# Sending a spectrum swap by halves of the frequencies, under an order of instructions searched one by one

## The chip, the cores and the metric

The kernel runs on one core of a Trainium2 chip. Times are device microseconds (us). With one core there is no second die to compare with; a run counts as slow when it is over 1.5% above the fastest of its kernel. Ratios are the mean time of one kernel's fast runs over the mean time of the other's fast runs of the same rounds, so they are not quite the ratios of the medians that stand beside them. The first comparison and three batches of experiments ran at different times, the batches on three chips; kernels of different batches are compared through their ratios to before. A +- beside such a difference is worked out from the two 95% intervals.

Engines are called TensorE (PE in the profile; PEld is its weight load), VectorE (DVE), ScalarE (ACT), GpSimd (POOL) and SyncE (SP, which issues the DMAs).

## The reference, cut to what matters

Two layers, each a gated long convolution (A) and an MLP (B), on x of 2048 x 512:

```python
def _A_ref(q, k, v, shift_k, ssm_k, ssm_D):
    k_shift = sum over 4 taps of k shifted in time * shift_k      # short filter
    kv = k_shift * v
    y = irfft(rfft(kv, 2*S) * rfft(ssm_k, 2*S))[:S] + kv * ssm_D   # long convolution over time
    return q * y
def _B_ref(x, w1, b1, w2, b2):
    return gelu(_layernorm(x) @ w1 + b1) @ w2 + b2

x = A_q
x = x + _A_ref(_layernorm(x), A_k, A_v, ...)   # y depends on k and v alone
x = x + _B_ref(_layernorm(x), ...)
x = x + _A_ref(_layernorm(x), A_k, A_v, ...)   # the same y again
x = x + _B_ref(_layernorm(x), ...)
```

The convolution y does not depend on x, so the kernel computes it once, in its first 90 us; the rest is the two MLPs.

## The kernel before: the parts that matter

A Python program lists about 1,080 operations with their data, and a list scheduler, at build time, puts them in an order on each engine and picks the engine of those that may run on ScalarE or VectorE (the evacuations of PSUM to SBUF). The order that it picks is then fixed: each engine runs its list in sequence and waits on semaphores.

The scheduler's knobs before: one bias per group of operations, and one reluctance of VectorE per group.

```python
    BIAS = {'fir0': 47900, 'fir1': -42700, ... 'z8': -60900}          # cut: one per group
    SHY = {'fir0': 1000, 'fir1': 150, 'h1': 950, ... 'z2': 1000}      # cut
    ...
            o.prio = o.base + o.extra + self.BIAS.get(o.tag, 0.0) + (1e9 - 1e5 * o.i if o.dma else 0.0)
```

The convolution is a two-stage Fourier transform made of matmuls. Stage 1 of the long filter (group h1), then stage 2 (h2), which leaves the filter's spectrum H with real parts in 64 partitions and imaginary parts in the other 64. A complex product also needs a copy HS with the two halves of the partitions exchanged. That copy is the *swap*: 4 MB from SBUF to SBUF, 16 DMAs of 256 KB.

```python
    P.tag = "h2"
    for k8 in range(16):                       # 8 of the 128 first-stage frequencies each
        tl = stage2(R_G, range(8 * k8, 8 * k8 + 8), 128)
        evac(BOTH, A(0, 128, R_H + 32 * k8, [4, 8], [512, 32], [1, 4]), ...)
    for d0, n in PARTS:                        # channels 0 to 63, 64 to 127
        for g in range(2):                     # upper half to lower, lower half to upper
            for c in range(0, 128 * n, 2048):
                src, dst = [A(64 * p, 64, r + 128 * d0 + c, [1, 2048]) for p, r in ((g, R_H), (1 - g, R_HS))]
                dma(dst, src, 1 << 18, reads=[src], rate=210.0)
```

A row of such a DMA (4096 bytes of one partition) holds all 128 frequencies, so no row can go before all 16 stage-2 evacuations are done. Meanwhile the short filter runs (fir0 and fir1 on TensorE, fir2 and fir3 as 16 multiplications and additions of 128x2048 on VectorE), then stage 1 of its result (x1), stage 2 (x2) and the products with H and HS on VectorE, 16 of 128x2048:

```python
            x = A(0, 128, xo, [0, 2], [4 * nk, n // 4], [1, 4 * nk])
            h = A(0, 128, R_H + 128 * d0 + 4 * k0, [R_HS - R_H, 2], [512, n // 4], [1, 4 * nk])
            tt(h, x, h, ALU.mult, 30 + 1.09 * w)        # reads H and HS: waits for the swap
```

The inverse stages (i1, i2) and the first normalisations lead to the MLP.

Of the kernel before, what the change touches and what calls it, by code (L numbers as in the profile page):

```python
# [12 lines left out]
PE, ACT, DVE, POOL, SP = "tensor", "scalar", "vector", "gpsimd", "sync"  # L13
# [25 lines left out]

class Op:  # L40
    __slots__ = ("i", "engs", "eng", "fn", "dur", "preds", "succ", "prio", "tile", "dma", "start", "end",
                 "pos", "inc", "waits", "val", "npred", "ready", "bytes", "base", "extra", "gate", "tag")


class Prog:
# [3 lines left out]

    G = 4  # L50
    LAT = 155.0
    BIAS = {'fir0': 47900, 'fir1': -42700, 'fir2': 66400, 'fir3': -218300, 'h1': 4900, 'h2': 147100, 'ht': 209900, 'i1_0': -157900, 'i1_64': 58800, 'i2_0': -83000, 'i2_64': -41700, 'm1': 127100, 'm2': -35800, 'q0': -48300, 'q1': 45200, 'q19': 14700, 'q2': -92900, 'q20': -190100, 'q21': 90800, 'q22': -36400, 'q3': -100900, 'q4': -92500, 'q5': 39100, 'q6': 114300, 'q7': 58300, 'q8': -27800, 'warm': -27900, 'warm0': 88600, 'x1_0': -97300, 'x1_1': 141900, 'x1_2': 44000, 'x1_3': -57400, 'x2_0': 149200, 'x2_64': 106500, 'y0': 55200, 'y1': 72900, 'y19': -31000, 'y2': 63100, 'y20': -119200, 'y21': 86900, 'y22': -58600, 'y3': -58100, 'y4': 64900, 'y5': 173000, 'y6': 55800, 'y7': -62200, 'y8': 8200, 'z0': 79600, 'z1': 62900, 'z19': 54600, 'z2': -30600, 'z20': 40700, 'z21': -55300, 'z22': -26300, 'z3': -7000, 'z4': 5000, 'z5': -87400, 'z6': -97200, 'z7': -15700, 'z8': -60900}
    SHY = {'fir0': 1000, 'fir1': 150, 'h1': 950, 'h2': 0, 'ht': 150, 'i1_0': 300, 'i1_64': 600, 'i2_0': 0, 'i2_64': 300, 'x1_0': 150, 'x1_1': 310, 'x1_2': 300, 'x1_3': 1000, 'x2_0': 360, 'x2_64': 1010, 'z0': 3000, 'z1': 600, 'z2': 1000}

    def __init__(self, nc):
        self.nc = nc
# [124 lines left out]
    def schedule(self):  # L181
        ops = self.ops
        n = len(ops)
        for o in ops:
            o.succ = []
            o.npred = len(o.preds)
            o.ready = 0.0
        for o in ops:
            for p in o.preds:
                ops[p].succ.append(o.i)  # L190
        for o in reversed(ops):
            d = o.dur if isinstance(o.dur, (int, float)) else min(o.dur.values())
            if o.dma:
                d += 2000.0 + o.bytes / 370.0
            b = 0.0
            for s in o.succ:
                b = max(b, ops[s].base + (0 if ops[s].engs == o.engs else self.LAT))
            o.base = b + d
            o.prio = o.base + o.extra + self.BIAS.get(o.tag, 0.0) + (1e9 - 1e5 * o.i if o.dma else 0.0)
        self.banks = [(0.0, []) for _ in range(8)]  # L200
        free = {e: 0.0 for e in (PE, ACT, DVE, POOL, SP)}
        ready = {e: [] for e in free}
        self.order = {e: [] for e in free}
        for o in ops:
            if o.npred == 0:
                for e in o.engs:
                    ready[e].append(o)
        done = 0
        dma_free = 0.0
        t = 0.0  # L210
        while done < n:
            best = None
            for e in free:
                te = max(free[e], 0.0)
                cand = None
                for o in ready[e]:
                    if o.eng is not None or any(g.eng is None for g in o.gate):
                        continue
                    s = max(te, o.ready)
                    new = [x for x in o.tile if x.base is None]  # L220
                    if any(x.pool.gate and self._gated(x) for x in new):
                        continue
                    if new:
                        pl = self._place(new, s)
                        if pl is None:
                            continue
                        s = pl[0]
                    k = (s + (self.SHY.get(o.tag, 300.0) if e == DVE and len(o.engs) > 1 and o.dur[DVE] > o.dur[ACT] else 0.0), -o.prio, o.i)
                    if cand is None or k < cand[0]:
                        cand = (k, o, s)  # L230
                if cand is None:
                    continue
                o = cand[1]
                d = o.dur if isinstance(o.dur, (int, float)) else o.dur[e]
                if best is None or (cand[0][0], cand[0][0] + d) < best[0]:
                    best = ((cand[0][0], cand[0][0] + d), e, o, cand[2])
            if best is None:
                raise RuntimeError("no op can be scheduled: %s" % [(o.i, e, [(t.base, t.left) for t in o.tile]) for e in ready for o in ready[e]][:10] + str((done, n)))
            _, e, o, s = best
            d = o.dur if isinstance(o.dur, (int, float)) else o.dur[e]  # L240
            o.eng, o.start = e, s
            new = [x for x in o.tile if x.base is None]
            if new:
                for tl, base in self._place(new, s)[1]:
                    tl.base = base
                    tl.pool.used += 1
                    for b in range(base, base + tl.pool.nb):
                        for p in self.banks[b][1]:
                            if p.i not in o.preds:
                                o.preds[p.i] = "psum"  # L250
                        self.banks[b] = None
            for tl in o.tile:
                tl.left -= 1
            free[e] = s + d
            if o.dma:
                dma_free = max(dma_free, s + d) + o.bytes / 370.0
                o.end = dma_free + 1900.0
            else:
                o.end = s + d
            for tl in o.tile:  # L260
                if tl.left == 0:
                    tail = [p for p in tl.ops if p.eng != PE] or [tl.ops[-1]]
                    tl.pool.used -= 1
                    for b in range(tl.base, tl.base + tl.pool.nb):
                        self.banks[b] = (max(p.end for p in tail) + self.LAT, tail)
            o.pos = len(self.order[e])
            self.order[e].append(o)
            for x in o.engs:
                ready[x].remove(o)
            for si in o.succ:  # L270
                q = ops[si]
                lat = self.LAT
                if not o.dma and len(q.engs) == 1 and q.engs[0] == o.eng:
                    lat = 0.0 if o.eng == PE or q.preds[o.i] == "psum" else 50.0
                q.ready = max(q.ready, o.end + lat)
                q.npred -= 1
                if q.npred == 0:
                    for x in q.engs:
                        ready[x].append(q)
            done += 1  # L280
        self.length = max(o.end for o in ops)
# [148 lines left out]
PARTS = ((0, 64), (64, 64))  # L430
# [5 lines left out]
def bass_interleave_layers__ssm_conv_h3__mixer_channel_mlp__prompt_kernel(  # L436
# [7 lines left out]
    def A(p0, n, off, *dims):  # L444
        return bass.AP(ar, p0 * AR + off, [[AR, n]] + [list(d) for d in dims])
# [16 lines left out]
    pos = [0]  # L462
# [17 lines left out]
    R_HRAW, R_HP, R_H = R_1, R_1 + 8192, R_1  # L480
    R_G, R_HS = R_4, R_2
# [19 lines left out]
    def dma(dst, src, nbytes, reads=(), prio=0.0, writes=None, eng=SP, rate=370.0):  # L501
        return P.op(eng, lambda e: e.dma_start(dst, src, allow_slow_non_contiguous=True), 550.0, reads=reads,  # L502
                    writes=[dst] if writes is None else writes, dma=True, nbytes=nbytes * 370 / rate, prio=prio)
# [34 lines left out]
    for i in range(NDV):  # L538
        o, s = A(0, 128, R_SJ + 512 * i, [128, 4], [1, 128]), A(0, 128, R_SR + 512 * DV_CH[i], [1, 4], [4, 128])
# [43 lines left out]
    for i, c in enumerate(PE_CH):  # L583
        o, a = A(0, 128, R_DG + i * 512, [128, 4], [1, 128]), A(0, 128, R_ID, [0, 4], [1, 128])
        tt(o, a, A(0, 128, R_SR + 512 * c, [1, 4], [4, 128]), ALU.mult, 1200.0, POOL)
    P.tag = "ht"
    for b in range(4):
        tl = Tile(dconv)
        src = [A(0, 128, R_HRAW + b * 2048 + a, [16, 128]) for a in range(16)]
# [8 lines left out]
        o = A(0, 1, R_HP + b * 2048, [64, 32], [1, 4])  # L598
# [33 lines left out]
    for k8 in range(16):  # L632
        tl = stage2(R_G, range(8 * k8, 8 * k8 + 8), 128)
        evac(BOTH, A(0, 128, R_H + 32 * k8, [4, 8], [512, 32], [1, 4]),
             lambda tl=tl: Q(tl, 0, 128, 0, [128, 8], [4, 32], [1, 4]), E1, tl)
    for d0, n in PARTS:
        for g in range(2):
            for c in range(0, 128 * n, 2048):
                src, dst = [A(64 * p, 64, r + 128 * d0 + c, [1, 2048]) for p, r in ((g, R_H), (1 - g, R_HS))]
                dma(dst, src, 1 << 18, reads=[src], rate=210.0)  # L640


    P.tag = ""

# [326 lines left out]
```

## Time and profile before

| what | before |
|---|---|
| time, median (first comparison, 4 runs) | 247.13 us |
| span of the profiled run | 245.5 us |
| first filter multiplication on VectorE (k has landed) | 17.44 us |
| swap issued from | 39.49 us |
| first MLP matmul | 89.06 us |
| TensorE busy from there to the end | 152.5 us of 156.4 us |

The page of before. The digits are the busy tenths of 40 slices of 6.1 us each:

```profile
span 245.5 us, 5643 instructions
## 1 busy us (share of the span) xinstructions
PE 228.3 (93%) x2382; PEld 154.6 (63%) x2399; DVE 175.1 (71%) x361; ACT 140.9 (57%) x222; POOL 34.1 (14%) x71
...
PE   7968789896799989999999999999999999999994
...
DVE  0759999999898898889999967998687203002233
ACT  2297898999898997665455343633265130872000
...
GB/s 240 372 408 406 406 47 82 215 212 212 346 396 198 0 3 0 45 43 3 46 43 43 3 41 67 24 1 21 101 53 0 109 19 43 45 0 43 43 45 85
```

Slices 15 and later are the MLPs, where TensorE is full. Slices 2 to 14 are the convolution, where three engines are nearly full. In slices 6 and 7 (31 to 43 us) the DMA rate drops to 47 and 82 GB/s: the loads are done and the swap cannot start. Then it runs at about 212 GB/s.

The DMA queue's own timeline of before (start, duration, queue, what, how many):

```profile
39.49 17.66 SPq L502 DMA_DIRECT2D ar<-ar  x16
```

VectorE's timeline of before: start, duration, what, and in brackets the idle time just before and what ended it. L513 is the helper of all SBUF multiplications and additions, L519 that of the evacuations:

```profile
17.44 6.90 DVE L513 TENSOR_TENSOR ar<-ar 128x2048 bf16<-128x2048 bf16 x6 [1.81 <-DMA ar<-in_A_k_dram]
...
53.29 9.16 DVE L513 TENSOR_TENSOR ar<-ar 128x2048 bf16<-128x2048 bf16 x8
63.63 9.17 DVE L513 TENSOR_TENSOR ar<-ar 128x2048 bf16<-128x2048 bf16 x8 [1.18 <-DMA ar<-ar]
...
79.10 1.23 DVE L519 CAST ar<-ps 128x1024 bf16<-128x1024 f32 x1 [0.45 <-PE ps L734]
81.32 0.69 DVE L519 CAST ar<-ps 128x512 bf16<-128x512 f32 x1 [1.00 <-PE ps L790]
```

So in 71 us VectorE stops for the swap once, for 1.18 us, at the start of the second part's products. The chain of waits, its shares of the span by engine:

```profile
PE 64%; DVE 12%; SPq 8%; DMA 8%; issue 2%; ACT 2%; POOL 1%
PE ps L897 31%; PE ps L930 30%; SPq L502 8%; DVE ar L513 8%; DMA ar<-in_A_k_dram 5%; DMA ar<-ar 3%; DVE ar L519 2%; ACT ar L518 2%; PE ps L734 1%; PE ps L919 1%; POOL sm L830 1%; DVE sm L822 1%; PE ps L790 1%; DVE ar L672 1%; PE ps L623 0%
```

Here the swap's issue and transfer (39.49 to 63.61 us) are a long stretch of the chain: 24.1 us, 9.8% of the span. (The page's 8% for SPq L502 also holds 4.6 us of load issues at the start, so its 8% and 3% must not be added up.)

Last, the busy times from the first filter multiplication to the first MLP matmul. The columns after the stretch and its length are the busy us of PE, PEld, DVE, ACT and POOL, then the clock, the DMA share and GB/s:

```profile
core 0: us, PE busy (x) PEld busy (x) DVE busy (x) ACT busy (x) POOL busy (x), PEclk, DMA share, GB/s
17.44:89.06 71.62, 61.97 (x1224) 55.39 (x1225) 68.17 (x89) 65.09 (x69) 6.42 (x14) 1.00 0.74 222
```

VectorE is busy 68.17 of 71.62 us, so idle 3.45 us (the listed waits and small gaps). ScalarE is idle 6.5 us, TensorE 9.7 us.

### The profile page before, as it was taken

How to read it: one execution, taken by the hardware profiler on the slowest of the kernel's cores; microseconds unless marked ns; L12 is line 12 of the kernel's file. 1: busy time of each engine (PE TensorE's matmuls, PEld its weight loads, DVE VectorE, ACT ScalarE, POOL GpSimd, SP SyncE). 2: the span in 40 equal slices, each digit the busy share in tenths (PEclk: the TensorE clock that was granted, in tenths of full speed). 3: DMA queues.
4: the chain of work that ended last, by engine and by line, in shares of the span. 5: the costliest groups of instructions: out<-in, count | busy, mean ns of one | idle time of the engine just before them, and what ended most of it. 6: DMA issues, size and time to landing. Idle time of an engine off the chain costs nothing.

```text
span 245.5 us, 5643 instructions
## 1 busy us (share of the span) xinstructions
PE 228.3 (93%) x2382; PEld 154.6 (63%) x2399; DVE 175.1 (71%) x361; ACT 140.9 (57%) x222; POOL 34.1 (14%) x71
## 2 busy tenths in 40 slices
PE   7968789896799989999999999999999999999994
PEld 3857779785689878776586666744444444444443
DVE  0759999999898898889999967998687203002233
ACT  2297898999898997665455343633265130872000
POOL 2320002000003031232231111102121000000000
PEclk9999999999999999999999999999999999999999
DMA  6999923999996000420222023101520501101112
GB/s 240 372 408 406 406 47 82 215 212 212 346 396 198 0 3 0 45 43 3 46 43 43 3 41 67 24 1 21 101 53 0 109 19 43 45 0 43 43 45 85
DMA packets 25770, 27.68 MB, mean 113 GB/s; under 512 B 17585, under 2 KB 19984, under 8 KB 25616
## 3 DMA queue, kind: packets, MB, share of 16 engines
q1 hardware_dynamic: 25598, 27.21, 37.8%
q8 instruction: 19, 0.31, 0.5%
q10 hardware_dynamic: 146, 0.10, 0.2%
q14 instruction: 7, 0.06, 0.1%
HBM read 17.34 MB, written 2.10 MB: 79 GB/s over the span
## 4 chain that ended last, share of the span: by engine, by line
PE 64%; DVE 12%; SPq 8%; DMA 8%; issue 2%; ACT 2%; POOL 1%
PE ps L897 31%; PE ps L930 30%; SPq L502 8%; DVE ar L513 8%; DMA ar<-in_A_k_dram 5%; DMA ar<-ar 3%; DVE ar L519 2%; ACT ar L518 2%; PE ps L734 1%; PE ps L919 1%; POOL sm L830 1%; DVE sm L822 1%; PE ps L790 1%; DVE ar L672 1%; PE ps L623 0%
## 5 line engine op out<-in xcount | busy, mean ns | idle before, releaser
L902 ACT ACTIVATE ar<-ps,sm 128x256 bf16<-128x256 f32 (+5 forms) x143 | 67.1, 524 | 69.5 <-PE ps L930 55.1
L897 PE MATMUL ps<-ar 128*128 128x256 bf16 (+4 forms) x569 | 79.7, 297 | 0.7 <-DVE ar L519 0.5
L930 PE MATMUL ps<-ar 128*128 128x512 bf16 (+1 forms) x327 | 74.4, 379 | 0.7
L518 ACT ACTIVATE ar<-ps 128x1024 bf16<-128x1024 f32 (+1 forms) x76 | 71.4, 1038 | 6.4 <-PE ps L610 2.9
L897 PEld LDWEIGHTS ps<-ar 128*128 128x128 bf16 (+1 forms) x572 | 53.2, 100 | 26.9 <-DVE ar L519 0.7
L513 DVE TENSOR_TENSOR ar<-ar 128x512 bf16<-128x512 bf16 (+2 forms) x104 | 61.9, 642 | 3.3 <-DMA ar<-in_A_k_dram 1.8
L930 PEld LDWEIGHTS ps<-ar 128*128 128x128 bf16 (+1 forms) x341 | 33.2, 98 | 37.5
L934 DVE TENSOR_TENSOR ar<-ar,ps 128x512 bf16<-128x512 bf16 x31 | 20.6, 681 | 44.8 <-PE ps L930 44.8
L822 DVE BATCH_NORM_STATS2 sm<-ar 128x6 f32<-128x512 bf16 (+1 forms) x68 | 41.8, 647 | 0.0
L837 DVE TENSOR_SCALAR ar<-ar,sm 128x512 bf16<-128x512 bf16 x64 | 23.5, 403 | 8.6 <-POOL sm L830 8.6
L830 POOL TENSOR_TENSOR sm<-sm 128x2 f32<-128x2 f32 (+2 forms) x26 | 20.2, 778 | 2.2
L610 PE MATMUL ps<-ar 128*64 128x128 bf16 x512 | 17.7, 221 | 2.7 <-ACT ar L518 1.9
L519 DVE CAST ar<-ps 128x1024 bf16<-128x1024 f32 (+1 forms) x16 | 17.9, 1149 | 3.1 <-PE ps L610 1.6
L828 POOL TENSOR_SCALAR sm<-sm 128x2 f32<-128x2 f32 (+2 forms) x26 | 5.7, 218 | 92.2 <-DVE sm L824 92.0
L734 PE MATMUL ps<-ar 128*128 128x128 bf16 x256 | 15.3, 220 | 3.0 <-DVE ar L513 1.6
L610 PEld LDWEIGHTS ps<-ar 128*64 128x64 bf16 x512 | 14.8, 110 | 5.1 <-ACT ar L518 3.0
L734 PEld LDWEIGHTS ps<-ar 128*128 128x128 bf16 x256 | 14.6, 114 | 3.6 <-DVE ar L513 1.7
L519 DVE COPY ar<-ps 128x2048 bf16<-128x2048 bf16 (+1 forms) x8 | 7.1, 917 | 6.8 <-PE ps L593 6.8
L710 PE MATMUL ps<-ar 128*128 128x64 bf16 x256 | 9.4, 193 | 1.9 <-ACT ar L518 1.1
L824 DVE BATCH_NORM_AGGREGATE sm<-sm 128x2 f32<-128x6 f32 (+1 forms) x64 | 10.3, 173 | 0.2
L710 PEld LDWEIGHTS ps<-ar 128*128 128x128 bf16 x256 | 8.1, 98 | 3.1 <-ACT ar L518 2.2
L623 PE MATMUL ps<-ar 128*128 128x128 bf16 x128 | 8.4, 220 | 1.5 <-ACT ar L518 1.0
(30 smaller groups left out, 77.5 us busy)
## 6 DMA issues: line engine op xcount, KB each, us to landing
ar<-tab_s SPq DMA_DIRECT2D x8, 512.0 KB, 16.1
ar<-ar SPq DMA_DIRECT2D x16, 256.0 KB, 6.5
ar<-in_A_ssm_k_dram SPq DMA_DIRECT2D x4, 512.0 KB, 5.4
ar<-in_A_k_dram SPq DMA_DIRECT2D x4, 512.0 KB, 10.1
ar<-in_A_v_dram SPq DMA_DIRECT2D x4, 512.0 KB, 13.6
ar<-in_A_q_dram SPq DMA_DIRECT2D x4, 512.0 KB, 9.0
out_dram<-ar SPq DMA_DIRECT2D x7, 256.0 KB, 2.0
ar<-in_B_w_dram SPq DMA_DIRECT2D x1, 1376.0 KB, 12.5
```

The lines of the kernel that those rows point to most:

```text
L513: return P.op(eng, lambda e: e.tensor_tensor(o, a, b, op), dur, reads=[a, b] + list(more), writes=[o])
L518: return e.activation(dst, src(), AF.Copy)
L519: return e.tensor_copy(dst, src())
L610: r = e.matmul(Q(tl, 64 * ri, 64, i * 128, [1, 128]), w, m, start=True, stop=True)
L734: r = e.matmul(Q(tl, 0, 128, i * 128, [1, 128]), w, m, start=q == 0, stop=q == 1)
L822: P.op(DVE, lambda e, sj=sj, x=x: e.bn_stats(sj, x), 40.0 + 1.1 * w, reads=[x], writes=[sj], gate=gate)
L830: P.op(POOL, lambda e: e.tensor_tensor(r, v, hf, ALU.pow), 430.0 + 150.0 * n, reads=[v, hf], writes=[r])
L837: P.op(DVE, lambda e: e.tensor_scalar(o, x, m, r, ALU.subtract, ALU.mult), 335.0, reads=[x, m, r], writes=[o])
L897: r = e.matmul(Q(tl, 0, rows, 0, [1, w]), a, m, start=dk == 0, stop=dk == 3)
L902: P.op(ACT, lambda e, dst=dst, tl=tl, rows=rows, bias=bias, w=w: e.activation(dst, Q(tl, 0, rows, 0, [1, w]), AF.Gelu_apprx_tanh, bias=bia ...
L930: r = e.matmul(Q(tl, 0, 128, 0, [1, 512]), ins[fc][0], ins[fc][1], start=fc == 0, stop=fc == 10)
L934: P.op(DVE, lambda e, x=x, tl=tl: e.tensor_tensor(x, x, Q(tl, 0, 128, 0, [1, 512]), ALU.add), 640.0, reads=[x], writes=[x], tile=tl)
```

## The change

Its intent: start the swap when half of the frequencies are there, and let a search choose the place, the engine and the reluctance of every single operation instead of one bias per group. The diff, cut to its core:

```diff
-    BIAS = {'fir0': 47900, 'fir1': -42700, ...
+    BIAS = {'': -535822, 'fir0': 990354, ...                  # cut
+    PB = {0: 776418, 1: 690696, 2: 999662841, ...             # a bias per operation; cut, about 1,000 entries
+    PS = {49: 175, 67: 1059, ...                              # cut
+    HOLD = {43: 10306, 51: 13509, ...                         # not before this planned time; cut, about 300 entries
+    ENG = {37: ('scalar',), 40: ('scalar',), 43: ('vector',), # the engine, for about 60 evacuations; cut
...
-            o.ready = 0.0
+            o.ready = self.HOLD.get(o.i, 0.0)
+            o.allow = self.ENG.get(o.i, o.engs)
...
-            o.prio = o.base + o.extra + self.BIAS.get(o.tag, 0.0) + (1e9 - 1e5 * o.i if o.dma else 0.0)
+            o.prio = o.base + o.extra + self.BIAS.get(o.tag, 0.0) + self.PB.get(o.i, 0.0) + (1e9 - 1e5 * o.i if o.dma else 0.0)
...
-    for d0, n in PARTS:
-        for g in range(2):
-            for c in range(0, 128 * n, 2048):
-                src, dst = [A(64 * p, 64, r + 128 * d0 + c, [1, 2048]) for p, r in ((g, R_H), (1 - g, R_HS))]
-                dma(dst, src, 1 << 18, reads=[src], rate=210.0)
+    for kh in range(2):
+        for d0, n in PARTS:
+            for c in range(0, 128 * n, 4096):
+                for g in range(2):
+                    o = 128 * d0 + c + 256 * kh
+                    src, dst = [A(64 * p, 64, r + o, [512, 8], [1, 256]) for p, r in ((g, R_H), (1 - g, R_HS))]
+                    dma(dst, src, 1 << 18, reads=[src], rate=210.0)
```

The 16 DMAs keep their 256 KB, but each now has 8 rows of 512 bytes per partition in place of one row of 4096. The tables take effect at build time only; at run time they are an order on each engine, a choice of engine and a choice of PSUM bank. The cut leaves out one more line of the scheduler: the time that it assumes from a transfer to its landing goes from 1900 to 2300 ns.

## The prediction

> **What bounds the kernel now.** The page gives PE 228.3 us busy of a 245.5 us span. By the table of 10 us windows the run has two parts. From 90 us to the end of the last matmul TensorE is 98.9% to 100% busy (the two MLPs, lines 897 and 930, 79.7 + 74.4 us of matmul); the chain of waits is nothing but those lines from 89.06 us to 242.5 us. No schedule can shorten that. Before 90 us (the convolution) TensorE is busy 76.8 us and idle about 13 us, VectorE is busy 76.3 us and ScalarE 73.7 us. From 17.4 us, where the first load of k has landed, to 89 us, the timeline leaves VectorE only about 3 us idle and ScalarE about 6 us. So the first part is bounded by evacuations and products on VectorE and ScalarE together. The change can only win out of those 13 us of TensorE idle time, of which 4 us lie before 20 us, where loads set the pace.
>
> **The swap.** Line 502's 16 swap DMAs are issued from 39.49 us, when the last stage-2 evacuation of the filter ends, to 55.9 us, one per about 1.2 us; the last lands at about 63.6 us. Meanwhile the DMA row shows the queues near empty from about 32 to 40 us, then 100% busy at only about 213 GB/s. A 4096-byte swap packet takes 0.325 us in the trace against 0.162 us for a load packet; I take the limit to be its ends (64 partitions to 64). VectorE waits for the swap only 1.18 us (at 63.63 us). The last tables, q and the MLP weights queue behind it and land at 66 to 78 us.
>
> After the change the first half can go when half of the stage-2 evacuations are done, about 34.5 us: 5 us sooner, into idle queues. The Trainium skill ("DMA: Bandwidth & Descriptors", Specifications) calls 512 B the least for line rate; the trace has 512-byte load packets at 27 ns, 75% of the large packets' rate per engine. Because swap packets already run at half rate (41 ns per 512 bytes), I expect the swap's rate nearly unchanged (180 to 215 GB/s). Last swap landing: about 56 to 59 us instead of 63.6; q and weights 5 us sooner. Direct gain: the 1.18 us wait, and freedom of order.
>
> **The order.** Busy times stay as they are (evacuation of 128x1024: 1.04 us ScalarE, 1.21 us VectorE). The search can fill TensorE's short stops (0.2 to 1.6 us each, about 9 us between 20 and 90 us), shift evacuations between engines and shorten the 82.2 to 89.06 us handover to the MLP. I expect 3 to 5 us of the 13 to be won: the MLP's steady part starts at about 85 us instead of 89.
>
> **Prediction.** 243.0 us, range 240.0 to 246.0. Chances: faster by over 2% 0.36, within 2% 0.61, slower 0.03.
>
> **What would show it.** TensorE busy stays at 228 +- 1 us; its idle time before the steady MLP falls by 3 to 5 us; the first swap DMA is issued before 36 us, in the 32 to 40 us hole; swap packets of 512 bytes take about 40 ns; VectorE's wait for the swap is gone; VectorE and ScalarE show over 95% in 20 to 85 us.
>
> **What would make it wrong.** 512-byte rows slow the swap (60 ns or more per packet), so the last half and the weights land later than now; or the searched order rests on durations that the chip does not keep, so waits only move; or it fills far more than I think (idle under 8 us, 240 us or less).

## The result, and the profile after

The changed kernel takes 244.44 us (median of 4 runs, 244.29 to 245.11) against 247.13 us; the ratio is 0.9893, 95% interval 0.9867 to 0.9919. It is faster by about 1%, within the 2% band. The profiled run is one with a clock of 0.993.

The page after:

```profile
span 242.7 us, 5658 instructions
## 1 busy us (share of the span) xinstructions
PE 229.0 (94%) x2399; PEld 155.7 (64%) x2399; DVE 176.1 (73%) x359; ACT 144.7 (60%) x224; POOL 32.8 (14%) x71
...
DVE  0459999999999998899999998797734760313022
ACT  2987899989998976755355444387004584005600
...
GB/s 236 361 407 406 407 107 206 194 195 241 398 376 47 0 3 0 45 44 23 24 45 0 46 2 64 68 0 45 45 71 18 43 43 22 68 43 86 0 57 76
```

The hole in the DMA rate is nearly closed (107 and 206 GB/s where 47 and 82 stood). The busy totals of the engines are the same within 4 us. The DMA queue's timeline after:

```profile
34.24 8.85 SPq L649 DMA_DIRECT2D ar<-ar  x8
43.13 0.72 SPq L649 DMA_DIRECT2D ar<-in_B_b_dram  x1
43.96 8.79 SPq L649 DMA_DIRECT2D ar<-ar  x8
```

The swap begins at 34.24 us, 5.25 us sooner. VectorE's timeline after (L660 is the old L513):

```profile
17.75 2.36 DVE L660 TENSOR_TENSOR ar<-ar 128x2048 bf16<-128x2048 bf16 x2 [2.44 <-DMA ar<-in_A_k_dram]
...
32.17 1.23 DVE L666 CAST ar<-ps 128x1024 bf16<-128x1024 f32 x1 [0.16 <-PE ps L770]
...
52.70 18.26 DVE L660 TENSOR_TENSOR ar<-ar 128x2048 bf16<-128x2048 bf16 x16
```

All 16 products run in one piece of 18.26 us; the wait for the swap is gone, and so are those at 79 and 81 us. The same stretch as before:

```profile
17.75:86.80 69.05, 62.11 (x1225) 56.96 (x1225) 68.07 (x90) 62.97 (x67) 5.46 (x14) 0.98 0.84 229
```

VectorE does the same 68.07 us of work in 69.05 us. Its idle time fell from 3.45 to 0.98 us, which makes 2.47 of the 2.57 us by which this stretch is shorter (71.62 - 69.05). ScalarE has less to do in it, 62.97 us in place of 65.09: in the new order it does more before k has landed (12.69 us busy in place of 8.14). The stretch began 0.31 us later, so the first MLP matmul came 2.26 us sooner, at 86.80 us. The remaining 0.5 us lies at the other end: from the first MLP matmul to the end of the span it takes 245.5 - 89.06 = 156.4 us before and 242.7 - 86.80 = 155.9 us after. The end of the timeline of before:

```profile
241.84 0.59 PE L930 MATMUL ps<-ar 128*128 128x512 bf16 x2
242.48 0.69 DVE L934 TENSOR_TENSOR ar<-ar,ps 128x512 bf16<-128x512 bf16 x1 [0.23 <-PE ps L930]
```

and of after, whose order ends on one of the half-width tiles that the program has for its last rows:

```profile
238.83 1.37 PE L1067 MATMUL ps<-ar 128*128 128x256 bf16 x11
...
240.24 0.42 DVE L1071 TENSOR_TENSOR ar<-ar,ps 128x256 bf16<-128x256 bf16 x1 [0.52 <-PE ps L1067]
```

Last addition 0.42 us in place of 0.69 us, and a smaller store behind it: from the last matmul's end to the end of the span, 245.5 - 242.45 = 3.1 us before, 242.7 - 240.21 = 2.5 us after.

### The profile page after: what moved, and what is told of

It reads as the page before. It is cut to its first block, busy times and chain, and to the rows that moved or that the text cites. A ratio compares the mean times of both kernels' runs of the same rounds, so it can differ in the third digit from the quotient of the medians.

```text
span 242.7 us, 5658 instructions
## 1 busy us (share of the span) xinstructions
PE 229.0 (94%) x2399; PEld 155.7 (64%) x2399; DVE 176.1 (73%) x359; ACT 144.7 (60%) x224; POOL 32.8 (14%) x71
## 4 chain that ended last, share of the span: by engine, by line
PE 69%; DVE 18%; DMA 5%; ACT 3%; SPq 2%; issue 1%; POOL 1%; DVEq 0%
PE ps L1045 32%; PE ps L1078 30%; DVE ar L660 11%; DMA ar<-in_A_k_dram 5%; DVE ar L666 4%; ACT ar L665 3%; PE ps L813 2%; SPq L649 2%; PE ps L757 2%; DVE sm L970 1%; PE ps L1067 1%; DVE ar L820 1%; PE ps L801 1%; DVE ar L985 1%; POOL sm L978 1%
## 5 line engine op out<-in xcount | busy, mean ns | idle before, releaser
L1050 ACT ACTIVATE ar<-ps,sm 128x256 bf16<-128x256 f32 (+5 forms) x143 | 68.0, 521 | 73.2 <-PE ps L1045 37.9
L1045 PE MATMUL ps<-ar 128*128 128x256 bf16 (+4 forms) x572 | 82.1, 297 | 0.0
L665 ACT ACTIVATE ar<-ps 128x1024 bf16<-128x1024 f32 (+2 forms) x78 | 74.3, 1059 | 10.0 <-PE ps L757 3.8
L1078 PE MATMUL ps<-ar 128*128 128x512 bf16 (+1 forms) x341 | 79.2, 379 | 0.0
L660 DVE TENSOR_TENSOR ar<-ar 128x512 bf16<-128x512 bf16 (+2 forms) x104 | 63.2, 645 | 3.1 <-DMA ar<-in_A_k_dram 2.4
L970 DVE BATCH_NORM_STATS2 sm<-ar 128x6 f32<-128x512 bf16 (+1 forms) x68 | 42.9, 649 | 0.4
L757 PE MATMUL ps<-ar 128*64 128x128 bf16 x512 | 18.9, 231 | 3.0 <-issue 1.1
L757 PEld LDWEIGHTS ps<-ar 128*64 128x64 bf16 x512 | 16.3, 117 | 5.0 <-ACT ar L665 1.9
L666 DVE CAST ar<-ps 128x1024 bf16<-128x1024 f32 (+1 forms) x17 | 19.2, 1151 | 0.3 <-PE ps L770 0.2
L666 DVE COPY ar<-ps 128x2048 bf16<-128x2048 bf16 (+1 forms) x5 | 4.5, 904 | 9.6 <-PE ps L740 9.5
```

Source lines behind the costliest of these rows:

```text
L660: return P.op(eng, lambda e: e.tensor_tensor(o, a, b, op), dur, reads=[a, b] + list(more), writes=[o])
L665: return e.activation(dst, src(), AF.Copy)
L666: return e.tensor_copy(dst, src())
L757: r = e.matmul(Q(tl, 64 * ri, 64, i * 128, [1, 128]), w, m, start=True, stop=True)
L970: P.op(DVE, lambda e, sj=sj, x=x: e.bn_stats(sj, x), 40.0 + 1.1 * w, reads=[x], writes=[sj], gate=gate)
L1045: r = e.matmul(Q(tl, 0, rows, 0, [1, w]), a, m, start=dk == 0, stop=dk == 3)
```

## The experiments

The tables of the search cannot be mixed: take the swap out of the new kernel, and the scheduler makes another order. So each kernel's order was frozen. The scheduler was replaced by a replay of a recorded list, which for each operation in turn gives the engine and the PSUM bank:

```diff
-    def schedule(self):
-        ...                                    # the list scheduler and its tables
+    def schedule(self):
+        for item in SEQ.split():               # "43D", "36P0", ...: operation, engine, PSUM bank
+            i, e, bases = re.match(r"(\d+)([A-Z])(\d*)", item).groups()
+            o, e = ops[int(i)], names[e]
+            ...                                # the same bookkeeping of banks and order, no choice
```

Compared at build time, the replay has the order on every engine, the banks and the semaphore waits of its original. The edits below leave order and banks as they are; those of the swap change four to six waits, of the swap and of the products that read it, and that of a_less moves one wait from one load to a later one. Names with b_ have the order of before, with a_ that of after. Each kernel ran five rounds beside before. All results are correct against the reference, also that of a_less, whose error is too small to be noticed.

The theory under test, called theory VectorE in the expectations: the length of the stretch from the first filter multiplication to the first MLP matmul is VectorE's work plus VectorE's idle time. Its rivals are the chain (the swap is worth what its share of the chain is), the order alone, and a bound shared by the engines.

### a_frozen: the changed kernel, replayed

No edit but the replay.

> The changed kernel with its order, engines and banks replayed from a fixed table instead of searched; the same instructions. It must give the time of the changed kernel, 244.4 us (0.989 of before). A difference over 0.3 us would mean that the runs of this batch cannot be compared with the first result.

Measured: 244.02 us (243.96 to 244.33, 4 runs) against 247.42, ratio 0.9859 (0.9834 to 0.9884). The instructions are those of after, whose first comparison gave 0.9893 (0.9867 to 0.9919). The intervals overlap, and the two ratios put the gain at 2.6 and 3.5 us. But the medians, 244.02 and 244.44 us, differ by more than the 0.3 us that the expectation allowed, so by that rule the first result is no yardstick for this batch. a_frozen is, and the a_ kernels below are compared with it and not with after.

### b_halves: only the swap by halves

```diff
 (the order of before, frozen; the new loop of 16 DMAs over kh, d0, c, g as in the change)
```

> The order of before, frozen; only the 16 swap transfers are cut by frequency halves. Theory VectorE (from the landing of k to the first MLP matmul the time is VectorE's work plus VectorE's own idle time, 2.9 us in before, of which the swap made 1.18 us): swap lands at 57 us or earlier, the wait at 63.6 us is gone, 1.0 to 1.2 us faster, 246.0 us. Rival chain theory (the page's chain puts 11% of the span on the swap, so 5 us earlier landing is worth most of 5 us): 243.5 us or less. Rival order theory (the swap is worth nothing, all is the search): 247.1 us.

Measured: 246.79 us (245.80 to 247.01), ratio 0.9958 (0.9933 to 0.9984), which is 1.0 us faster. The swap begins at 34.86 us, and the wait is gone:

```profile
53.13 18.25 DVE L486 TENSOR_TENSOR ar<-ar 128x2048 bf16<-128x2048 bf16 x16
```

The theory VectorE had said 1.0 to 1.2 us. The chain reading falls: the swap makes 24.1 us of the chain, starts 4.6 us sooner and lands 3.3 us sooner (60.27 in place of 63.61 us), yet no more comes back than about the 1.18 us by which VectorE waited for it. The interval is wide (0.4 to 1.7 us): two of the six runs took 245.8 to 245.9 us, the profiled one among them, and four took 246.7 to 247.0.

### a_whole: only the searched order

```diff
 (the order of after, frozen; the old loop of 16 DMAs over d0, g, c, rows of 4096 bytes)
```

> The order of after, frozen; the swap in whole rows again, which must wait for the last stage-2 evacuation (about 41 us in the trace of after). Theory VectorE: the swap lands at about 65 us, VectorE reaches the products of the second part at 61.9 us and waits about 3 us, so about 3 us slower than after, 247.4 us: the searched order needs the halves. Rival order theory: 244.5 us, no loss. Additive theory (the swap is worth the same 1.2 us in both orders): 245.6 us.

Measured: 247.49 us (247.09 to 248.00), ratio 0.9997 (0.9973 to 1.0022): the searched order without the halves is worth nothing. VectorE waits for the swap twice:

```profile
53.88 9.17 DVE L486 TENSOR_TENSOR ar<-ar 128x2048 bf16<-128x2048 bf16 x8 [1.55 <-DMA ar<-ar]
64.71 9.17 DVE L486 TENSOR_TENSOR ar<-ar 128x2048 bf16<-128x2048 bf16 x8 [1.65 <-DMA ar<-ar]
```

That makes 3.2 us, as expected, although as two waits and not as one. With b_halves this fills a table of two by two; each cell is the ratio to before:

| | swap whole | swap by halves |
|---|---|---|
| order of before | 1 | 0.9958 |
| order of after | 0.9997 | 0.9859 |

The halves are worth 1.0 us in the old order and 3.4 us in the new one (0.0138 of 247.4 us). The order is worth 0.1 us without the halves and 2.4 us with them. The parts are not additive: if they were, both together would give 0.9958 + 0.9997 - 1 = 0.9955, and the measured 0.9859 is lower by 0.0096, with some 0.004 of uncertainty. The reason is in the waits: the new order reaches the products sooner, which pays only if the swap is there.

### b_rows512: only the rows of 512 bytes

```diff
 (the order of before, frozen)
+    for d0, n in PARTS:
+        for kh in (1, 0):                      # the later half first: waits for the last evacuation, as before
+            for c in range(0, 128 * n, 4096):
+                for g in range(2):             # rows of 512 bytes, as in the change
```

> The order of before, frozen; rows of 512 bytes, but the later half of the frequencies is sent first within each part, so the swap starts when it did in before (39.5 us). It measures the row size alone. If packets at half rate hide the descriptor cost: last landing 63 to 64 us as before and 247.1 us. If 512-byte rows cost what they cost a load (27 ns against 20 ns per 512 bytes, a third more): the swap takes 30 us instead of 24, VectorE waits some 6 us more, 253 us.

Measured: 249.31 us (248.76 to 249.73), ratio 1.0068 (1.0046 to 1.0090): this loop costs 1.7 us (1.1 to 2.2). The truth lies between the two expectations. The loop differs from that of before in the rows and also in the sequence: it changes direction with every transfer, where before sends four of one direction and then four of the other. The two were not run apart, so that the rows are the cause is likely and not shown. The table of windows of b_rows512, in mid-swap:

```profile
48.00:52.00 4.00, 3.45 (x100) 2.97 (x101) 3.95 (x4) 4.00 (x6) 0.00 (x0) 1.00 1.23 196
52.00:56.00 4.00, 3.29 (x97) 2.92 (x94) 3.04 (x4) 3.01 (x4) 0.00 (x0) 1.00 1.22 196
```

and of before in the same windows:

```profile
48.00:52.00 4.00, 3.38 (x99) 2.88 (x98) 3.95 (x4) 4.00 (x6) 0.00 (x0) 1.00 1.01 214
52.00:56.00 4.00, 3.43 (x104) 3.05 (x101) 4.00 (x5) 4.00 (x5) 0.00 (x0) 1.00 1.04 207
```

The last column is GB/s: 196 against 207 to 214, about 7% less. From first issue to last landing the swap takes 25.65 us (39.41 to 65.06) in place of 24.12. In the trace's packet records a 512-byte packet of the swap takes 0.047 us, where an eighth of a 4096-byte one takes 0.325 / 8 = 0.041 us. In this order the swap gates VectorE:

```profile
54.24 9.17 DVE L486 TENSOR_TENSOR ar<-ar 128x2048 bf16<-128x2048 bf16 x8 [0.96 <-DMA ar<-ar]
65.14 9.18 DVE L486 TENSOR_TENSOR ar<-ar 128x2048 bf16<-128x2048 bf16 x8 [1.72 <-DMA ar<-ar]
```

These are waits of 2.68 us in place of one of 1.18, so the slower rate is paid in full. In the order of after no wait for the swap is left to pay it.

### a_dve2, b_dve2: more work for VectorE

```diff
-               more=halo if j else ())
+               more=halo if j else (), twice=i == 1 and j in (1, 2))   # two multiplications of fir3 done twice
```

> The order of after, frozen; two multiplications of the filter on VectorE (128x2048, 1.15 us each) are done twice, the result is unchanged. Theory VectorE (VectorE is busy without a gap from 17.75 us to 86.7 us): the whole 2.3 us (plus at most 0.2 us for two waits of VectorE for itself) is added, 246.8 us. Rival (TensorE and ScalarE share the bound): 245.5 us or less.

> The order of before, frozen; the same two multiplications done twice. Theory VectorE: the wait for the swap, 1.18 us at 63.6 us, absorbs as much, so only 1.1 to 1.3 us is added, 248.3 us. If the swap did not gate VectorE in before: 249.4 us.

Measured: a_dve2 246.38 us, ratio 0.9940 (0.9921 to 0.9959), which is 2.0 us (+- 0.8) above a_frozen; b_dve2 249.28 us, ratio 1.0064 (1.0042 to 1.0087), 1.6 us (+- 0.6) above before. In before the wait for the swap shrank from 1.18 to 0.45 us, so it took up 0.7 us of the 2.3, less than I had said: one of the two repeats stands before the start of the swap, and the swap itself began later, at 40.97 us.

### a_act2: more work for ScalarE

```diff
-        return P.op(engs, f, durs, writes=[dst], tile=tile)
+        return P.op(engs, f, durs, writes=[dst], tile=tile, twice=P.tag == "x1_2" and dst.offset % 16 == 0)
```

(Two of the four evacuations of that group meet the condition.)

> The order of after, frozen; two evacuations on ScalarE (128x1024, 1.0 us each, at about 42 us) are done twice. Theory VectorE: ScalarE has idle time of its own (about 3 us between 28 and 87 us) but gates VectorE through TensorE; most of the 2.0 us is absorbed, 244.4 to 245.2 us. Rival (VectorE and ScalarE are both at the bound): 246.4 us.

Measured: 245.42 us (245.20 to 247.53), ratio 0.9921 (0.9892 to 0.9951), 1.5 us (+- 1.0) above a_frozen, between the two expectations. The profiled run is the slowest of the six, with a clock of 0.985, so I read nothing else from it; without it the difference is 1.2 us.

### a_pe2, b_pe2: more work for TensorE

```diff
-                for ri, i, w, m in ins:
+                for ri, i, w, m in ins * (2 if tag == "x1_2" else 1):    # stage 1 of one channel group, twice
```

> The order of after, frozen; the first-stage matmuls of one channel group (64 of 128x128 onto 64 columns, 2.3 us of TensorE in all) are done twice at about 39 to 45 us. Theory VectorE: TensorE still has stops there; 1.5 us or more of it is absorbed, below 245.2 us. Rival (TensorE is the bound everywhere, as its 94% busy time says): 246.7 us.

> The order of before, frozen; the same first-stage matmuls of TensorE done twice (2.3 us). After paid all of it (+2.4 us). If the idle time of TensorE in before was free to be filled, as my prediction took it: below +1 us, 248.2 us or less. If TensorE's stops there are hand-overs that move with the work: +1.5 us or more, 248.7 us or more; a part can vanish in the wait for the swap.

Measured: a_pe2 246.66 us, ratio 0.9956 (0.9932 to 0.9981), 2.4 us (+- 0.9) above a_frozen; the stretch is 1.93 us longer (70.88 against 68.95 us, both at a clock of 1.0). The 2.3 us are the scheduler's figure of 37 ns a matmul. In the trace of a_frozen 80 such matmuls in a row take 2.44 us, about 30 ns each, so that the added 64 take an estimated 1.9 us. By either figure the added work is paid in full or nearly, against my expectation. b_pe2 247.51 us, ratio 0.9997 (0.9970 to 1.0024): the same work is free in the order of before, within 0.7 us. By the test that the expectation set, TensorE's idle time in before was free to be filled, as the prediction took it. What VectorE waited for in b_pe2:

```profile
50.59 1.23 DVE L492 CAST ar<-ps 128x1024 bf16<-128x1024 f32 x1 [0.25 <-PE ps L583]
52.42 2.36 DVE L492 CAST ar<-ps 128x1024 bf16<-128x1024 f32 x2 [0.61 <-PE ps L583]
...
64.19 9.17 DVE L486 TENSOR_TENSOR ar<-ar 128x2048 bf16<-128x2048 bf16 x8 [0.33 <-ACT ar L491]
```

VectorE did lose 1.05 us to TensorE (0.25 and 0.61 us here, and 0.19 us at 45.5 us), but ahead of the swap: where before had waited 1.18 us for the swap, 0.33 us of waiting was left, now for ScalarE. VectorE's idle time in the stretch rose only from 3.45 to 3.60 us. The rest of the added work went into TensorE's own stops, of which 9.65 us were there. In a_pe2 there is no such cushion:

```profile
44.09 1.22 DVE L646 TENSOR_TENSOR ar<-ps,ar 128x1024 bf16<-128x1024 f32 x1 [0.63 <-PE ps L639]
67.12 5.81 DVE L486 TENSOR_TENSOR ar<-ar 128x2048 bf16<-128x2048 bf16 x5 [0.95 <-ACT ar L491]
```

The delay comes out as two new waits, and the idle time rose from 0.92 to 2.50 us. The searched order has spent the slack that was there.

### a_less: less work for VectorE

```diff
         def tap(j, o):
-            tt(o, A(0, 128, R_K + (3 - j) * 512 + 128 * c, [512, 16], [1, 128]), ...
+            n = 1 if i == 1 and j > 1 else 16       # one sixteenth of the columns: wrong on purpose
+            tt(o[:, :n], A(0, 128, R_K + (3 - j) * 512 + 128 * c, [512, n], [1, 128]), ...
```

> The order of after, frozen; two multiplications of the filter on VectorE do one sixteenth of their columns (1.15 us becomes about 0.15 us each; the result is wrong on purpose). If VectorE alone is the bound: 2.0 us faster than after, 242.2 us. If the three engines hold each other (as the three doubled costs suggest, each of which was paid in full or nearly): less than 1 us faster, 243.3 us or more.

Measured: 243.88 us (243.67 to 244.50), ratio 0.9849 (0.9824 to 0.9874), against 0.9859 for a_frozen: 0.2 us (+- 0.9) faster, which cannot be told from zero and is clearly less than 2 us. The stretch, and VectorE's products in it:

```profile
17.74:86.80 69.06, 62.47 (x1224) 57.08 (x1225) 66.75 (x90) 63.11 (x68) 5.42 (x14) 0.98 0.83 229
```

```profile
51.52 12.64 DVE L486 TENSOR_TENSOR ar<-ar 128x2048 bf16<-128x2048 bf16 x11
64.31 2.36 DVE L486 TENSOR_TENSOR ar<-ar 128x2048 bf16<-128x2048 bf16 x2 [0.16 <-ACT ar L491]
66.86 2.36 DVE L486 TENSOR_TENSOR ar<-ar 128x2048 bf16<-128x2048 bf16 x2 [0.18 <-ACT ar L491]
69.61 1.23 DVE L486 TENSOR_TENSOR ar<-ar 128x2048 bf16<-128x2048 bf16 x1 [0.38 <-ACT ar L491]
```

VectorE's work fell from 68.03 to 66.75 us and its idle time rose from 0.92 to 2.31 us; the length stayed. (Two shorter multiplications should take 2.0 us off. The rest is hidden in the records: the four evacuations after them take 4.95 us in place of 4.62, the 16 products 18.6 in place of 18.3.) VectorE reaches the products about 1.1 us sooner after the landing of k than in a_frozen, and loses that lead before they end, 0.72 us of it in waits for ScalarE, which evacuates the products' inputs. One caution: the granted clock was 0.66 from 62 to 66 us in this run, and ScalarE waited for TensorE there (0.39 and 0.60 us), so some of these waits may be the dip's. The conclusion does not hang on this profile: the one run at a clock of 1.0 took 243.67 us, the two of a_frozen 243.96 and 244.03. So the theory VectorE is right as bookkeeping and wrong as a cause in the new order: VectorE is not the bound there alone.

### The stretch in all kernels

From the table of windows; T0 is the first filter multiplication, T1 the first MLP matmul, idle is T1 - T0 less the busy time (us). The profiles of after, a_whole, b_rows512 and a_less have a dip of the clock in the stretch (0.98 in the mean); that of a_act2 (0.95) and the two spoiled a_load kernels are left out:

| kernel | T0 | T1 | T1 - T0 | VectorE busy | VectorE idle | span - T1 |
|---|---|---|---|---|---|---|
| before | 17.44 | 89.06 | 71.62 | 68.17 | 3.45 | 156.4 |
| b_halves | 17.29 | 87.67 | 70.38 | 68.07 | 2.31 | 156.4 |
| b_rows512 | 17.35 | 90.56 | 73.21 | 68.25 | 4.96 | 156.3 |
| b_dve2 | 17.66 | 91.03 | 73.37 | 70.58 | 2.79 | 156.4 |
| b_pe2 | 17.67 | 89.62 | 71.95 | 68.35 | 3.60 | 156.4 |
| after | 17.75 | 86.80 | 69.05 | 68.07 | 0.98 | 155.9 |
| a_frozen | 17.38 | 86.33 | 68.95 | 68.03 | 0.92 | 155.9 |
| a_whole | 17.52 | 89.69 | 72.17 | 68.08 | 4.09 | 155.9 |
| a_dve2 | 17.73 | 88.68 | 70.95 | 70.30 | 0.65 | 155.9 |
| a_pe2 | 18.03 | 88.91 | 70.88 | 68.38 | 2.50 | 155.9 |
| a_less | 17.74 | 86.80 | 69.06 | 66.75 | 2.31 | 155.9 |

T0 wanders by 0.7 us between runs, since it depends on the loads. The last column shows no dependence on the swap: it is 156.3 to 156.4 us in the old order and 155.9 us in the new one, in each of the kernels.

### a_load, a_load2: an attempt at a faster kernel, which failed

Every engine waits for k to land at about 17.4 us. I tried to make that sooner.

```diff
-    dma(A(0, 128, R_SR, [1, 2048]), dr(A_shift_k, 0, [0, 128], [1, 2048]), 1 << 19)
+    dma(A(0, 128, R_SR + 1024, [1, 1024]), dr(A_shift_k, 1024, [0, 128], [1, 1024]), 1 << 18)
...
+        if step == "k":                             # after k: 2 KB of taps for the two TensorE groups
+            dma(A(0, 128, R_SD, [4, NPE], [1, 4]), dr(A_shift_k, 0, [4, 128], [512, NPE], [1, 4]), 2048)
...
-        tt(o, a, A(0, 128, R_SR + 512 * c, [1, 4], [4, 128]), ALU.mult, 1200.0, POOL)
+        tt(o, a, A(0, 128, R_SD + 4 * i, [1, 4], [0, 128]), ALU.mult, 1200.0, POOL)
```

a_load2 also moves the load of the long filter's last quarter behind k, with its transposition, evacuation and first stage.

> The order of after, frozen; the filter taps are sent to all partitions for two channel groups only (256 KB less before k), and the other two groups' taps come as 2 KB after k. Theory VectorE (its gapless stretch begins when k has landed, 17.4 to 17.8 us): k lands 0.6 us sooner and the whole 0.6 us is won, 243.5 us. If the start of the stretch does not matter: 244.1 us.

> As a_load, and the last quarter of the long filter is loaded after k; its transposition, evacuation (now on ScalarE) and first stage come later in the order. k lands about 1.9 us sooner than in after. Theory VectorE: 1.2 to 1.9 us faster than after, 242.2 to 242.9 us. Rival (ScalarE and TensorE are at the bound too and get the same work later): no better than a_load, 243.5 us or more.

Measured: a_load 249.65 us, ratio 1.0077 (1.0052 to 1.0102); a_load2 253.58 us (four fast runs, 252.57 to 255.35; two slow ones, 257.48 and 257.66, left out), ratio 1.0259 (1.0216 to 1.0302). Both are slower, and through a mistake of mine. GpSimd in a_load:

```profile
9.85 0.42 POOL L497 TENSOR_TENSOR ar<-ar 1x128 bf16<-1x128 bf16 x1 [1.41 <-ACT ar L502]
17.73 2.65 POOL L497 TENSOR_TENSOR ar<-ar 128x512 bf16<-128x512 bf16 x3 [7.46 <-DMA ar<-in_A_shift_k_dram]
```

The small load stands behind k in the queue, and GpSimd's fixed order has its consumers ahead of two small additions that the first stage of the long filter needs. TensorE then waited 7.12 us for GpSimd (in a_load2 4.32 and 3.26 us). The 2 KB should have gone before k. What an earlier k is worth stays open; these two runs say nothing about it, only that an order frozen for one arrival of data punishes another.

## Why the prediction was right or wrong, point by point

**The sum was about right.** 243.0 us was predicted with a range of 240.0 to 246.0; 244.44 us was measured, and 244.02 us in the second comparison. "Within 2%" was the likelier of the three and came true. A part of that is luck: 0.5 us of the gain came from the end of the kernel, where the prediction had said that nothing could be won.

**"The change can only win out of those 13 us of TensorE idle time ... I expect 3 to 5 us of the 13 to be won": the term that was mis-sized.** TensorE's idle time before the first MLP matmul went from 89.06 - 75.86 = 13.2 us to 86.80 - 75.61 = 11.2 us, by 2.0 us (by 1.4 us in a_frozen, whose stretch had a clock of 1.0). The narrower pool was VectorE's: the stretch held 3.45 us of its idle time, with 68 us of work that the change does not shorten, and 2.5 us of those were won. TensorE's idle time is no such pool. b_pe2 shows that work could be put into it for nothing; that does not make the stretch shorter. In before 5.3 of the 9.7 us that TensorE is idle in the stretch are waits for ScalarE's evacuations (among them regular gaps of 0.28 us), 2.7 us are waits for VectorE. The Trainium skill ("Trainium Kernel Development and Optimization", Best Practices) says to mind PSUM pressure, because tiling on TensorE speeds up the matmuls but not the evacuation of PSUM. No run here changes the tiling; what the trace shows is that ScalarE, which does nothing but evacuate PSUM in this stretch, is busy 62.97 of 69.05 us after the change.

**"The MLP's steady part starts at about 85 us instead of 89": wrong by that term.** It starts at 86.80 us.

**"No schedule can shorten that" (the part after 89 us): wrong by 0.5 us.** The searched order ends on a half-width tile; span less T1 fell from 156.4 to 155.9 us.

**"Direct gain: the 1.18 us wait": right, and shown.** b_halves won 1.0 us (0.4 to 1.7). But the sentence took the two parts of the change as separate. In the searched order the halves are worth 3.4 us, because a_whole waits 3.2 us for the swap.

**"I expect the swap's rate nearly unchanged (180 to 215 GB/s)" and packets of about 40 ns: right in kind, off in size.** The rate was about 195 GB/s against 207 to 214, inside the range; the packets took 47 to 48 ns. b_rows512 priced it at 1.7 us where the swap gates. The expected last landing, 56 to 59 us, was therefore a little early: in after it is at 60.51 us, 3.1 us sooner than in before (63.61) though the swap starts 5.25 us sooner. "q and weights 5 us sooner" was wrong: the last part of q landed at 71.5 us as before (71.4), the last weights at 75.1 in place of 78.6 us.

**"VectorE and ScalarE show over 95% in 20 to 85 us": right for VectorE, at the edge for ScalarE.** VectorE is busy 64.19 of 65 us (98.8%), ScalarE 61.81 us (95.1%, 93.9% in the replay at a clock of 1.0).

**What held the gain to 1%.** The old order had a cushion, VectorE's wait for the swap; in b_pe2 0.85 of the 1.05 us that VectorE lost to TensorE vanish in it. The change removed it and filled most of VectorE's other gaps. After that, added work is paid on TensorE (2.4 +- 0.9 us for an estimated 1.9 to 2.3), on VectorE (2.0 +- 0.8 of 2.3 us) and mostly on ScalarE (1.5 +- 1.0 of 2.0 us), while less work for VectorE wins nothing measurable. I read this as three engines that hold each other, so that only an order that takes work or waits from several of them at once could go on. That VectorE alone is not the bound is shown. Less work for ScalarE or for TensorE was not run, so that neither of them alone is the bound is argued from the doubled costs; which buffer or dependence couples them at each point was not tried.

**What stays open.** Which of the search's thousand entries matter: only the order as a whole was tested. Whether an earlier landing of k would be worth its full time: a_load was spoiled. Whether a layout in which half of the frequencies are contiguous, so that the halves keep rows of 4096 bytes, would gain anything in the new order: not run; since VectorE does not wait for the swap there, I would estimate little.

## What to carry to other kernels

Size a reordering by the idle time of the engine that has the most work in the stretch, not by the idle time of the engine that one would like to see full; and do not read a chain's share as a gain, since the next chain takes over as soon as the wait is gone (24 us of chain, 1.0 us). Splitting a transfer and searching the order belong together: each alone gave 1.0 and 0.1 us, both gave 2.6 to 3.5. When an order has been searched until no engine has slack, freeze it and add a known cost on each engine in turn: what is paid in full shows that the slack is spent there, and where taking work away wins nothing, that engine alone is not the bound.

## What the Trainium skill lacked or had wrong

- "DMA: Bandwidth & Descriptors", Why small descriptors are slow (HBM only): it says that SBUF to SBUF transfers do not suffer from small descriptors. Here rows of 512 bytes, sent in alternating directions, ran the swap at 196 GB/s against 207 to 214 with rows of 4096 bytes, 47 ns against 41 ns per 512 bytes, and cost the kernel 1.7 us.
- The same page, Specifications: it gives 512 bytes as the least for line rate. In this trace 512-byte load packets take 27 ns, and 4096-byte ones 162 ns, so 19 and 25 GB/s per engine: three quarters of the rate.
- "SBUF — State Buffer", Door 1: The DMA port swizzle: its asymptote of 218 GB/s for 64 partitions agrees with the 207 to 214 GB/s of the swap. But the row of the page's Summary that gives 436 GB/s for SBUF to SBUF does not repeat that condition; for the swap, which goes from one half of the partitions to the other, 436 is twice what was measured.
- No page says how to put a number on a change of order where several engines are nearly full. The runs here show that in such a stretch the same 64 matmuls (an estimated 1.9 to 2.3 us) can cost nothing (ratio 0.9997) or everything (2.4 us), depending on the order.
